# Last stage of a gated attention/SSM mix in 64 by 64 matmul tiles, and its tail ordered by a planner

## The chip, the cores and the metric

The kernel runs on one core of one Trainium2 chip. The metric is the device time of one execution in microseconds (us). Engines are called as in the profile: PE (TensorE matmuls; PEld are its weight loads), DVE (VectorE), ACT (ScalarE), POOL (GpSimd) and SP (SyncE); SP and POOL issue nearly all the transfers.

## The reference, cut to what matters

```python
g = sigmoid((x * gate_w).sum(-1, keepdims=True))    # one gate per token
a = local_dilated_attention(x, wqkv, wo)            # 32 heads, window 8, step 2
# b: per channel, a convolution over the 2048 tokens with a kernel K of that channel
K = einsum("dn,dnl,dn->dl", C, exp(dt*A*l), dt*B).real
y = irfft(rfft(pad(x)) * rfft(pad(K)))[:2048]
b = y + x * Dskip
out = g * a + (1 - g) * b                           # 2048 tokens x 640 channels, bf16
```

## The kernel before

The first part, to 299 us of the profiled span, computes the attention, stores `g*a` in device memory (`gaS`) and `1-g` (`omS`), makes K and the first half of the Fourier transforms of K and x. Its tasks are ordered by `Plan` (L69): each task has an engine, an estimated duration, inputs (`deps`), buffer slots that it takes and gives back (`acq`, `rel`) and a due time; `order()` plays them through and `emit()` records the instructions of each engine in that order.

The second part, `fft_conv` (L988), was written in program order. It multiplies the spectra and transforms back, all by matmuls with constant matrices:

- **Products** (L1013 to L1042), eight blocks of four frequencies. Per block four groups of eight matmuls give the real and imaginary part of both spectra into `fp` (L1023, two PSUM buffers of four banks); ACT evicts each into `sp_*` (L1026); DVE forms the complex product with six operations of 1280 elements per partition, four multiplications into `ta` and `tb_` and two additions into `Y` (L1036 to L1042). In the last block the imaginary part goes in three pieces of 16, 32 and 32 columns, so that the next stage can begin. SP loads the constants PSI and the input `gaF`; a two-element copy on POOL that reads a spectrum (L1004) holds each of the first loads back.
- **First inverse step** (`inv`, L1050): 20 results `cp` of 16 matmuls on 64-row tiles, alternately copied by ACT (L982) and DVE (L984) into `C`.
- **Last stage** (L1068 to L1090): 16 results `yp`. A partition is one of four channel groups (160 channels) times 32 tokens; a result holds four token steps. Per step two matmuls on the whole array, 128 x 160 (L1076). Then `(1-g)` scales: on DVE for six results (L1081), on ACT for ten, in four ACTIVATEs each (L1086). DVE adds `g*a` (L1087). Two results make an output tile `ot` (four buffers), stored by four transfers of 32 partitions in rows of 160 channels, 320 B (L1090).

DVE's order in the last stage, as recorded, is three scalings, eight adds, three scalings, eight adds. The results of both stages share four PSUM slots of two banks (tag `cy`). Two engines never read one result there.

Of the kernel before, what the change touches and what calls it, by code (L numbers as in the profile page):

```python
# [10 lines left out]
ACT = mybir.ActivationFunctionType  # L11
# [57 lines left out]
class Plan:  # L69
# [3 lines left out]
             "at": 2, "asb": 2, "pv": 2, "oT": 1, "ga": 1, "prj": 4, "prjw": 3, "pc": 4}  # L73
# [133 lines left out]
class Attn:  # L207
# [45 lines left out]
    def plan_gate(self, pl, cst, pa, g_sb, late):  # L253
# [25 lines left out]
        def twice(_):  # L279
            b["om2"] = cst.tile([16, 128, 2], BF16, name="om2")  # L280
            nc.scalar.activation(b["om2"][:], b["gz"][0:16, 1, 0:128].unsqueeze(2).to_broadcast([16, 128, 2]), ACT.Identity)

        def store(_):
            nc.gpsimd.dma_start(self.omS.rearrange("(i p) t -> i (p t)", p=128), b["om2"][:].rearrange("i p t -> i (p t)"))
# [5 lines left out]
        w = pl.add("gtwice", "A", 0.35, twice, deps=[u], rel=[("ar", m)], due=d)  # L290
# [621 lines left out]
def _fft_consts():  # L912
# [6 lines left out]
    for g in range(4):  # L919
        f1b[g, :, g, :] = f1c.reshape(32, 64)  # L920
# [14 lines left out]
    psis = np.zeros((32, 4, 64, 2, 4, 32), np.float32)  # L935
    for g in range(4):
        psis[:, g, :, 0, g, :] = Psi.real.transpose(1, 0, 2)
        psis[:, g, :, 1, g, :] = -Psi.imag.transpose(1, 0, 2)
    psis = psis.reshape(128, 64, 2, 128)
# [3 lines left out]
def fft_prefetch(ctx, tc, x, omS):  # L943
# [6 lines left out]
    P["omF"] = pre.tile([128, 64, 2], BF16, name="omF")  # L950
# [20 lines left out]
    def gates(g):  # L971
        nc.gpsimd.dma_start(P["omF"][32 * g:32 * g + 32], omS.rearrange("(a b) t -> a b t", b=64))
# [15 lines left out]
def fft_conv(ctx, tc, P, big, Bu, gaS, out2d):  # L988
# [4 lines left out]
    Bk = bufA[:].rearrange("p (c f q g) -> p c f q g", c=NCH, f=64, q=8)  # L993
    sb = ctx.enter_context(tc.tile_pool(name="ff_sb", bufs=1))
    Y = sb.tile([128, 2, 80, 128], BF16, name="Y")
    yv = Y[:].rearrange("p r x (f g) -> p r x f g", g=4)
    om32 = sb.tile([128, 64], F32, name="om32")
    psr = ctx.enter_context(tc.tile_pool(name="ff_psr", bufs=1))
    psis = []

    def load_psi(k, pool, after=None):
        t = pool.tile([128, 8, 2, 128], BF16, name=f"PSI{k}")
        if after is not None:
            nc.gpsimd.tensor_copy(t[:, 0, 0, 0:2], after)  # L1004
        nc.sync.dma_start(t[:], psi_d[:, 8 * k:8 * k + 8])
        psis.append(t)
    with big:
        nc.vector.tensor_copy(om32[:], omF[:, :, 0])
        gaF = P["pool"].tile([128, 64, 160], BF16, name="gaF", tag="uga")
        gr = gaS.rearrange("(a b) d -> a b d", b=64)  # L1010
        phis = P["phis"]
        with tc.tile_pool(name="ff_wk", bufs=2, side="right") as wk, tc.tile_pool(name="ff_ps2", bufs=2, space=PSUM) as ps2:
            for fb in range(8):  # L1013
                spec = {}
                PHI = phis[fb]
                for nm, B in (("k", Bk), ("u", Bu)):
                    for ro in range(2):
                        fp = ps2.tile([128, 4, 512], F32, name="fp")
                        for fl in range(4):
                            f1 = 4 * fb + fl  # L1020
                            for ri in range(2):
                                kind = (0 if ri == 0 else 2) if ro == 0 else (1 if ri == 0 else 0)
                                nc.tensor.matmul(fp[:, fl, 0:320].rearrange("p (c x) -> p c x", x=32), PHI[:, fl, kind, :],  # L1023
                                                 B[:, :, 2 * f1 + ri].rearrange("p c q g -> p c (q g)"), start=(ri == 0), stop=(ri == 1))
                        t = wk.tile([128, 80, 4, 4], BF16, name=f"sp_{nm}{ro}")
                        nc.scalar.activation(t[:], fp[:, :, 0:320].rearrange("p f (x g) -> p x f g", g=4), ACT.Identity)  # L1026
                        spec[(nm, ro)] = t
                if fb + 3 < 8:
                    phis.append(P["load_phi"](fb + 3))
                if fb < 4:  # L1030
                    load_psi(fb, psr, spec[("u", 1)][:, 0, 0, 0:2])
                    nc.sync.dma_start(gaF[32 * fb:32 * fb + 32], gr[:, :, 160 * fb:160 * fb + 160])
                ur, ui, kr, ki = spec[("u", 0)], spec[("u", 1)], spec[("k", 0)], spec[("k", 1)]
                ta = wk.tile([128, 80, 4, 4], BF16, name="ta")
                tb_ = wk.tile([128, 80, 4, 4], BF16, name="tb_")
                nc.vector.tensor_tensor(ta[:], ur[:], kr[:], ALU.mult)  # L1036
                nc.vector.tensor_tensor(tb_[:], ui[:], ki[:], ALU.mult)
                nc.vector.tensor_tensor(yv[:, 0, :, 4 * fb:4 * fb + 4, :], ta[:], tb_[:], ALU.subtract)
                for x0, x1 in (((0, 16), (16, 48), (48, 80)) if fb == 7 else ((0, 80),)):
                    nc.vector.tensor_tensor(ta[:, x0:x1], ur[:, x0:x1], ki[:, x0:x1], ALU.mult)  # L1040
                    nc.vector.tensor_tensor(tb_[:, x0:x1], ui[:, x0:x1], kr[:, x0:x1], ALU.mult)
                    nc.vector.tensor_tensor(yv[:, 1, x0:x1, 4 * fb:4 * fb + 4, :], ta[:, x0:x1], tb_[:, x0:x1], ALU.add)  # L1042
    C = bufA[:].rearrange("p (x d) -> p x d", d=160)
    with tc.tile_pool(name="ff_ps3", bufs=4, space=PSUM) as ps3, tc.tile_pool(name="ff_psr2", bufs=1, side="right") as psr2, \
            tc.tile_pool(name="ff_wk2", bufs=4, side="right") as wk2:
        for k in range(4, 8):
            load_psi(k, psr2)
        cps = {}

        def inv(cb, ro):  # L1050
            if ro == 0:
                cps[cb] = ps3.tile([128, 2, 4, 128], F32, name="cp", tag="cy")
            cp = cps[cb]
            for l in range(4):
                for c2 in range(2):
                    nc.tensor.matmul(cp[:, c2, l, :], Y[64 * c2:64 * c2 + 64, ro, 4 * cb + l, :],
                                     GAB[64 * c2:64 * c2 + 64, ro, :], start=(ro == 0 and l == 0), stop=(ro == 1), skip_group_check=True, tile_position=(64 * c2, 0))
            if ro == 1:
                dst = C.rearrange("p x (c q) -> p x c q", c=2)[:, :, :, 4 * cb:4 * cb + 4]
                copy_on(nc, 0 if cb == 9 else cb, dst, cp[:].rearrange("p c l x -> p x c l"))  # L1060
        for cb in range(4):
            inv(cb, 0)
        for cb in range(20):
            if cb >= 4:
                inv(cb, 0)
            inv(cb, 1)
        orr = out2d.rearrange("(a b) d -> a b d", b=64)
        for tb8 in range(8):  # L1068
            tt = wk2.tile([128, 8, 160], BF16, name="tt")
            ot = wk2.tile([128, 8, 160], BF16, name="ot")  # L1070
            for hh in range(2):
                yp = ps3.tile([128, 2, 512], F32, name="yp", tag="cy")
                for l in range(4):
                    t2 = 8 * tb8 + 4 * hh + l
                    for ro in range(2):
                        nc.tensor.matmul(yp[:, l // 2, 160 * (l % 2):160 * (l % 2) + 160], psis[tb8][:, 4 * hh + l, ro, :], C[:, 64 * ro + t2, :],  # L1076
                                         start=(ro == 0), stop=(ro == 1))
                t0 = 8 * tb8 + 4 * hh
                th = tt[:, 4 * hh:4 * hh + 4]
                if (2 * tb8 + hh) % 5 in (1, 3):  # L1080
                    nc.vector.tensor_tensor(th.rearrange("p (a b) (d t) -> p a b d t", b=2, t=2),  # L1081
                                            yp[:, :, 0:320].rearrange("p a (b d t) -> p a b d t", b=2, t=2),
                                            omF[:, t0:t0 + 4, :].rearrange("p (a b) t -> p a b t", b=2).unsqueeze(3).to_broadcast([128, 2, 2, 80, 2]), ALU.mult)
                else:
                    for l in range(4):
                        nc.scalar.activation(th[:, l], yp[:, l // 2, 160 * (l % 2):160 * (l % 2) + 160], ACT.Identity, scale=om32[:, t0 + l:t0 + l + 1])  # L1086
                nc.vector.tensor_tensor(ot[:, 4 * hh:4 * hh + 4], th, gaF[:, t0:t0 + 4, :], ALU.add)  # L1087
            for g in range(4):
                eng = (nc.sync, nc.gpsimd, nc.sync, nc.scalar if tb8 == 7 else nc.gpsimd)[g]
                eng.dma_start(orr[:, 8 * tb8:8 * tb8 + 8, 160 * g:160 * g + 160], ot[32 * g:32 * g + 32])  # L1090
# [182 lines left out]
```

## Time and profile before

| | us |
|---|---|
| time of 3 runs | 378.54, 380.16, 382.12 (median 380.16) |
| profiled execution, its own time | 382.15 |
| its span | 380.4 |
| busy: PE, DVE, ACT, POOL | 319.4, 323.0, 307.8, 92.6 |
| blocks of products begin | 299.1 |
| last input spectrum evicted | 342.1 |
| copies of the first inverse step | 345.5 to 357.7 |
| first matmul of the last stage | 357.8 |
| first store issued, last store issued | 363.6, 374.7 |

The span counts from the first to the last instruction; the time of the execution is 1.75 us longer. "Busy" of PE is of pipelined matmuls, whose durations overlap: the pitch of a matmul (the length of a row of n matmuls by n) is its cost, not its duration.

### The profile page before, as it was taken

To read this page: it belongs to the slowest core of one execution; us is meant where nothing else is said; L and a number is where in the kernel's file an instruction comes from. 1 tells how busy PE (TensorE), PEld (TensorE's weight loads), DVE (VectorE), ACT (ScalarE), POOL (GpSimd) and SP (SyncE) were. 2 spreads that over 40 slices of the span, in tenths; PEclk is the share of its full clock that TensorE was granted. 3 is DMA by queue.
4 is the path that set the end of the run, shared out by engine and by line. 5 is a ranking of instruction groups with operands and counts; after the bars stand their busy time and mean duration, and the time that the engine had idled before them with its cause. 6 is when DMAs were issued, how large, how long until landed. Compare 5 with 4: busy or idle time off the path is not lost.

```text
span 380.4 us, 11537 instructions
## 1 busy us (share of the span) xinstructions
PE 319.4 (84%) x4938; PEld 190.8 (50%) x4966; DVE 323.0 (85%) x435; ACT 307.8 (81%) x433; POOL 92.6 (24%) x122
## 2 busy tenths in 40 slices
PE   0259999998999999979898989999999899978760
PEld 0135663533454455444444535566777665547750
DVE  4788999768999788998999998999896299999772
ACT  1598884489998889898989879987986799995890
POOL 8930341130103031573520201000010022000053
PEclk9998999999999999986969989999999999998995
DMA  8991898671426359426647733222461299915056
GB/s 264 371 254 36 254 277 243 167 242 57 149 68 194 125 138 244 107 56 152 153 103 211 252 96 113 73 73 58 161 209 36 67 202 234 234 15 214 2 138 142
DMA packets 51528, 58.83 MB, mean 155 GB/s; under 512 B 36244, under 2 KB 43284, under 8 KB 51220
## 3 DMA queue, kind: packets, MB, share of 16 engines
q1 hardware_dynamic: 41492, 28.78, 28.6%
q0 software_dynamic: 8256, 28.69, 25.7%
q8 instruction: 39, 0.64, 0.7%
q10 hardware_dynamic: 1728, 0.61, 0.7%
q14 instruction: 13, 0.11, 0.1%
HBM read 38.29 MB, written 19.77 MB: 153 GB/s over the span
## 4 chain that ended last, share of the span: by engine, by line
PE 29%; ACT 16%; DVE 7%; issue 3%; POOL 1%; DMA 1%; POOLq 0%; ACTq 0%; DVEq 0%
PE tb L449 6%; PE fp L1023 5%; PE bp L1194 5%; ACT big L784 5%; PE tb L466 4%; PE ar L772 3%; ACT sp_u L1026 3%; DVE bufA L984 3%; ACT sp_k L1026 3%; PE kps L825 2%; PE yp L1076 2%; ACT big L786 1%; ACT bufA L784 1%; POOL out_dram L1090 1%; DVE prod L379 1%
## 5 line engine op out<-in xcount | busy, mean ns | idle before, releaser
L330 PE MATMUL tb<-bufA 128*128 128x512 bf16 x283 | 71.6, 389 | 4.5 <-DVE bufA L494 2.0
L772 PE MATMUL ar<-Rarg,L 64*128 64x304 bf16 (+1 forms) x480 | 56.0, 289 | 10.5 <-ACT big L784 4.2
L784 ACT ACTIVATE big<-ar 128x608 bf16<-128x608 int16 x96 | 58.3, 682 | 3.2 <-PE ar L772 2.6
L786 ACT ACTIVATE big<-ar 128x864 bf16<-128x864 f32 x60 | 49.4, 895 | 1.2 <-PE ar L772 1.0
L444 DVE TENSOR_TENSOR pv<-vc,asb 128x2048 bf16<-128x2048 bf16 x40 | 47.4, 1220 | 3.3 <-PE tb L449 3.3
L379 DVE TENSOR_TENSOR prod<-qc,kc 128x2048 bf16<-128x2048 bf16 x40 | 47.5, 1220 | 3.1 <-PE lg L385 3.1
L330 PEld LDWEIGHTS <-bufA 128*128 128x128 bf16 x300 | 33.2, 120 | 31.9 <-issue 7.4
L772 PEld LDWEIGHTS <-L 64*128 64x128 bf16 x480 | 22.0, 95 | 41.7 <-issue 37.2
L449 PE MATMUL tb<-pv,ident 128*128 128x512 bf16 (+1 forms) x181 | 39.7, 357 | 1.0 <-issue 0.5
L825 PE MATMUL kps<-qq,pt 128*32 128x22 bf16 (+1 forms) x2560 | 37.0, 174 | 1.7 <-issue 1.5
L825 PEld LDWEIGHTS <-pt 128*32 128x32 bf16 (+1 forms) x2560 | 25.1, 93 | 25.5 <-issue 17.1
L1023 PEld LDWEIGHTS <-PHI 128*128 128x128 bf16 x256 | 24.8, 97 | 17.6 <-issue 7.4
L466 PE MATMUL tb<-wo_sb,oT 128*128 128x320 bf16 x160 | 28.0, 307 | 0.0
L492 ACT ACTIVATE prj<-tb 128x512 bf16<-128x512 f32 x27 | 16.0, 598 | 13.4 <-PE tb L330 13.0
L449 PEld LDWEIGHTS <-ident 128*128 128x128 bf16 x192 | 18.1, 101 | 14.4 <-issue 2.2
L1026 ACT ACTIVATE sp_k<-fp 128x1280 bf16<-128x1280 f32 x16 | 19.1, 1236 | 3.3 <-PE fp L1023 3.3
L809 DVE TENSOR_TENSOR qq<-big 128x1408 bf16<-128x1408 bf16 x24 | 21.2, 885 | 0.0
L245 PE MATMUL ar<-ident,xn 128*128 128x128 bf16 x80 | 7.9, 263 | 15.9 <-DMA xn<-in_A_x_dram 14.2
L1023 PE MATMUL fp<-bufA,PHI 128*128 128x320 bf16 x128 | 19.1, 298 | 2.2 <-ACT sp_u L1026 1.5
L1023 PE MATMUL fp<-big,PHI 128*128 128x320 bf16 x128 | 19.2, 298 | 1.8 <-ACT sp_k L1026 1.8
L1026 ACT ACTIVATE sp_u<-fp 128x1280 bf16<-128x1280 f32 x16 | 19.1, 1237 | 1.8 <-PE fp L1023 1.8
L370 POOL DMA_DIRECT2D vc<-vS x8 | 7.0, 880 | 48.2 <-DVE pv L444 39.5
(198 smaller groups left out, 610.0 us busy)
## 6 DMA issues: line engine op xcount, KB each, us to landing
asb<-aS SPq DMA_DIRECT2D x8, 512.0 KB, 4.0
PSI<-c_psi SPq DMA_DIRECT2D x8, 512.0 KB, 6.0
PHI<-c_phi POOLq DMA_DIRECT2D x8, 384.0 KB, 5.7
Sprm<-pc SPq DMA_DIRECT2D x12, 240.0 KB, 7.8
L<-Sprm SPq DMA_DIRECT2D x80, 36.0 KB, 2.6
kc<-kS POOLq DMA_DIRECT2D x8, 337.5 KB, 6.2
vc<-vS POOLq DMA_DIRECT2D x8, 337.5 KB, 5.6
xn<-in_A_x_dram SPq DMA_DIRECT2D x4, 640.0 KB, 11.7
```

What stands on the lines that cost most here:

```text
L330: nc.tensor.matmul(ppf, self.wq[:, kt, which * D + e:(which + 1) * D:5], self.xT[:, c0 // 1024, kt, c0 % 1024:c0 % 1024 + SC], start=(kt = ...
L379: nc.vector.tensor_tensor(b[e][:], b["qc"][:, e, :].unsqueeze(1).to_broadcast([128, W, C]), win(b["kc"][:, e, :], 0, W, DIL, C), ALU.mult)
L444: nc.vector.tensor_tensor(b["pv", e][:, :, k, :].rearrange("p w (b t) -> p w b t", t=64), for_e, aw, ALU.mult)
L449: nc.tensor.matmul(b["op", e][:, 0:n, :], ident[:], b["pv", e][:, w, 0:n, :], start=(w == 0), stop=(w == W - 1))
L466: nc.tensor.matmul(apf[:, :320], b["oT"][:, e, i * 128:(i + 1) * 128], wo_sb[:, e, hf * 320:(hf + 1) * 320], start=(e == 0), stop=(e == 4))
L772: nc.tensor.matmul(ar[:, g2, a0:a0 + ncol], L[rows, sb, gp, l0:l0 + 128], R[rows, c0:c0 + ncol], start=True, stop=True, tile_position=(64 ...
L784: nc.scalar.activation(dst[:, 2 * gp:2 * gp + 2, sub, :], ar[:].bitcast(I16)[:, :, 0:2 * SW:2], ACT.Sin, scale=SCL)
L786: nc.scalar.activation(dst[:, 2 * gp:2 * gp + 2].rearrange("p g s n -> p g (s n)"), ar[:, :, 0:2 * EW], ACT.Exp)
L809: nc.vector.tensor_tensor(qq[:], trg[:, :, KI:].rearrange("p a (v m) -> p a v m", v=2), exq[:, :, KI:].unsqueeze(2).to_broadcast([128, 32, ...
L825: nc.tensor.matmul(kps[32 * g:32 * g + 32, h, NM * ql:NM * ql + NM], pt[rows, k, v, :], qq[rows, k, v, :], start=(g not in started), stop= ...
L1023: nc.tensor.matmul(fp[:, fl, 0:320].rearrange("p (c x) -> p c x", x=32), PHI[:, fl, kind, :], B[:, :, 2 * f1 + ri].rearrange("p c q g -> p ...
L1026: nc.scalar.activation(t[:], fp[:, :, 0:320].rearrange("p f (x g) -> p x f g", g=4), ACT.Identity)
```

## The change

The last stage works on 64 by 64 tiles. A partition is now one of two token halves (of 32 steps each) times two channel halves times 32 tokens, and the two groups of 160 channels of a half lie in the two banks of a result: 32 token steps with 320 channels per partition instead of 64 steps with 160. A step takes eight matmuls of 64 rows, 64 columns and 160 moving elements, on the four 64 by 64 tiles of the array. The constants are half as large (one tile `psi`), and the rows of `omS`, `gaF` and of the output change with it: an output row is now 320 channels, 640 B. For this the order of the four channel groups in the constant F1c is permuted, `Y` is laid out with the group ahead of the frequency, and the eviction of `fp` reads the four frequencies of a column, which lie in four banks, one after another.

A result has three steps (the last has two; there are 11), with four slots. For its first step DVE scales and adds in one operation, out of PSUM; for the other steps ACT scales, one ACTIVATE of 320 elements per step, and DVE adds both in one operation. An output tile holds two results, but results 0, 9 and 10 have one each; it is stored by two transfers of SP and two of POOL.

In the products, both multiplications with the real part of the input come first, then the two with the imaginary part, each followed by its addition; in the last block these go in the three pieces. All of `fft_conv` is made of tasks of the planner, which chooses the engine of the 20 copies (ACT or DVE) too. The gate `1-g` is no longer stored twice per token. The recorded order of the first part stays as it was.

```diff
-            nc.scalar.activation(b["om2"][:], b["gz"][0:16, 1, 0:128].unsqueeze(2).to_broadcast([16, 128, 2]), ACT.Identity)
+            nc.scalar.activation(b["om2"][:], b["gz"][0:16, 1, 0:128], ACT.Identity)
...
-        f1b[g, :, g, :] = f1c.reshape(32, 64)
+        f1b[g, :, (0, 2, 1, 3)[g], :] = f1c.reshape(32, 64)
...
-    yv = Y[:].rearrange("p r x (f g) -> p r x f g", g=4)
+    yv = Y[:].rearrange("p r x (g f) -> p r (x g) f", g=4)
...
+    pl = Plan(free=dict(P=0.0, A=0.0, D=0.0, S=0.0, G=0.0), phase=0.0, look=0.0, ba=0.0, bd=0.0, grace=0.0, warm=1)
...
-                        t = wk.tile([128, 80, 4, 4], BF16, name=f"sp_{nm}{ro}")
-                        nc.scalar.activation(t[:], fp[:, :, 0:320].rearrange("p f (x g) -> p x f g", g=4), ACT.Identity)
+                t = wk.tile([128, 320, 4], BF16, name=f"sp_{nm}{ro}")
+                evict(nc, en, t[:], spec[nm, ro][:, :, 0:320].rearrange("p f x -> p x f"))
...
+        for ro in range(2):
+            last = pl.add(f"ta{fb}{ro}", "D", 0.81, lambda _, f=mul, ro=ro: f(_, 0, 80, f"ta{ro}", ("u", 0), ("k", ro)), deps=[sp["u", 0], sp["k", ro]], after=[last], due=d - 1)
+            heads.append(last)
+        for k, (x0, x1) in enumerate(((0, 16), (16, 48), (48, 80)) if fb == 7 else ((0, 80),)):
+            w = 0.04 + 0.0096 * (x1 - x0)
+            for ro in range(2):
+                p1 = pl.add(f"tc{fb}{k}{ro}", "D", w, lambda _, f=mul, x=(x0, x1), ro=ro: f(_, x[0], x[1], "tc", ("u", 1), ("k", 1 - ro)), deps=[sp["u", 1], sp["k", 1 - ro]], after=[last], due=d + k)
+                last = pl.add(f"Y{fb}{k}{ro}", "D", w, lambda _, f=add, x=(x0, x1), ro=ro: f(_, x[0], x[1], ro), deps=[heads[ro], p1], due=d + k)
...
+        cps.append(pl.add(f"cp{cb}", "AD", {"A": 1.0, "D": 1.18}, ev, deps=ms, rel=[("cy", ms[0])], due=60 + cb))
+    for n, w in enumerate((3,) * 10 + (2,)):
...
-                        nc.tensor.matmul(yp[:, l // 2, 160 * (l % 2):160 * (l % 2) + 160], psis[tb8][:, 4 * hh + l, ro, :], C[:, 64 * ro + t2, :],
-                                         start=(ro == 0), stop=(ro == 1))
+            for k, v in enumerate(vs):
+                for ro in range(2):
+                    for j in range(2):
+                        for h in range(2):
+                            nc.tensor.matmul(yp[64 * j:64 * j + 64, h, 160 * k:160 * k + 160], psi[64 * h:64 * h + 64, 32 * j + v, ro, :], C[64 * h:64 * h + 64, 64 * ro + 32 * j + v, :],
+                                             start=(ro == 0), stop=(ro == 1), skip_group_check=True, tile_position=(64 * h, 64 * j))
...
-                        nc.scalar.activation(th[:, l], yp[:, l // 2, 160 * (l % 2):160 * (l % 2) + 160], ACT.Identity, scale=om32[:, t0 + l:t0 + l + 1])
-                nc.vector.tensor_tensor(ot[:, 4 * hh:4 * hh + 4], th, gaF[:, t0:t0 + 4, :], ALU.add)
+        def scale(_, v, k, n=n, part=part):
+            nc.scalar.activation(q["tt", n][:, k - 1, :].rearrange("p (h d) -> p h d", h=2), part(k), ACT.Identity, scale=om32[:, v:v + 1])
+        def mix(_, n=n, vs=vs, o=o, k0=k0):
+            nc.vector.tensor_tensor(o["t"][:, k0 + 1:k0 + w, :], q["tt", n][:, 0:w - 1, :], gaF[:, vs[1]:vs[0] + w, :], ALU.add)
+        def both(_, v=vs[0], o=o, k0=k0, part=part):
+            nc.vector.scalar_tensor_tensor(o["t"][:, k0, :].rearrange("p (h d) -> p h d", h=2), part(0), om32[:, v:v + 1], gaF[:, v, :].rearrange("p (h d) -> p h d", h=2), ALU.mult, ALU.add)
...
-                eng.dma_start(orr[:, 8 * tb8:8 * tb8 + 8, 160 * g:160 * g + 160], ot[32 * g:32 * g + 32])
+                for h in range(2):
+                    j = (0, 2)[e == "G"] + h
+                    (nc.sync if e == "S" else nc.gpsimd).dma_start(orr[j // 2, j % 2][:, o["v"]:o["v"] + o["n"], :], o["t"][32 * j:32 * j + 32, 0:o["n"]])
```

The lines of the changed kernel that the prediction names: L1021 (matmuls of `fp`), L492 and L494 (evictions and copies by the common helper `evict`, L490), L1048 and L1051 (multiplications, additions into `Y`), L1075 (`cp`), L1105 (`yp`), L1114 (ACT's scaling), L1118 and L1121 (DVE's add and its combined operation), L1132 (stores).

More of the change, by code (lines that the diff above doesn't have):

```diff
@@ L289, in plan_gate @@
         u = pl.add("gturn", "P", 0.1, turn, deps=[v], due=d, eq=20)
-        w = pl.add("gtwice", "A", 0.35, twice, deps=[u], rel=[("ar", m)], due=d)
+        w = pl.add("gtwice", "A", 0.25, row, deps=[u], rel=[("ar", m)], due=d)
         pl.add("gst", "G", 0.55, store, deps=[w], due=d, dma=0.4)
@@ L949, in fft_prefetch @@
     P["GAB"] = pre.tile([128, 2, 128], BF16, name="GAB")
-    P["omF"] = pre.tile([128, 64, 2], BF16, name="omF")
+    P["omF"] = pre.tile([128, 32], BF16, name="omF")
     P["pace"] = pre.tile([128, 2], BF16, name="pace")
@@ L993, in fft_conv @@
     Bk = bufA[:].rearrange("p (c f q g) -> p c f q g", c=NCH, f=64, q=8)
+    C = bufA[:].rearrange("p (x d) -> p x d", d=160)
     sb = ctx.enter_context(tc.tile_pool(name="ff_sb", bufs=1))
     Y = sb.tile([128, 2, 80, 128], BF16, name="Y")
-    yv = Y[:].rearrange("p r x (f g) -> p r x f g", g=4)
[L997 to L1024, printed above, removed]
-                        t = wk.tile([128, 80, 4, 4], BF16, name=f"sp_{nm}{ro}")
-                        nc.scalar.activation(t[:], fp[:, :, 0:320].rearrange("p f (x g) -> p x f g", g=4), ACT.Identity)
-                        spec[(nm, ro)] = t
-                if fb + 3 < 8:
-                    phis.append(P["load_phi"](fb + 3))
[L1030 to L1042, printed above, removed]
@@ new lines, in fft_conv @@
+    yv = Y[:].rearrange("p r x (g f) -> p r (x g) f", g=4)
+    om32 = sb.tile([128, 32], F32, name="om32")
+    psi = sb.tile([128, 64, 2, 64], BF16, name="psi")
+    nc.vector.tensor_copy(om32[:], omF[:])
+    gaF = P["pool"].tile([128, 32, 320], BF16, name="gaF", tag="uga")
+    gr = gaS.rearrange("(a j v) (e c) -> j e a v c", j=2, v=32, e=2)
+    orr = out2d.rearrange("(a j v) (e c) -> j e a v c", j=2, v=32, e=2)
+    phis, q = P["phis"], {}
+    a, b, c = ExitStack(), ExitStack(), ExitStack()
@@ new lines, in fft_conv, with inv, ev @@
+    cps, prev = [], None
+    for cb in range(20):
+        ms = []
+        for ro in range(2):
+            def inv(_, cb=cb, ro=ro):
+                if cb == 0 and ro == 0:
+                    b.close()
+                    q["ps"] = c.enter_context(tc.tile_pool(name="ff_ps3", bufs=4, space=PSUM))
+                if ro == 0:
+                    q["cp", cb] = q["ps"].tile([128, 2, 4, 128], F32, name="cp")
+                for l in range(4):
+                    for c2 in range(2):
+                        nc.tensor.matmul(q["cp", cb][:, c2, l, :], Y[64 * c2:64 * c2 + 64, ro, 4 * cb + l, :],
+                                         GAB[64 * c2:64 * c2 + 64, ro, :], start=(ro == 0 and l == 0), stop=(ro == 1), skip_group_check=True, tile_position=(64 * c2, 0))
+            prev = pl.add(f"inv{cb}{ro}", "P", 0.27, inv, deps=[muls[cb, ro]], after=ends + [prev], acq=["cy"] if ro == 0 else [], due=60 + cb + 0.1 * ro)
+            ms.append(prev)
+        def ev(en, cb=cb):
+            evict(nc, en, C.rearrange("p x (c q) -> p x c q", c=2)[:, :, :, 4 * cb:4 * cb + 4], q["cp", cb][:].rearrange("p c l x -> p x c l"))
+        cps.append(pl.add(f"cp{cb}", "AD", {"A": 1.0, "D": 1.18}, ev, deps=ms, rel=[("cy", ms[0])], due=60 + cb))
```

136 lines of the change are left out of this document (84 added, 52 removed).

## Prediction

> **What bounds the kernel now.** The page's chain of waits comes first. TensorE (PE) leads with 29% of the span and no line has more than 6%, so only the stage that is edited can be costed. The table by stage comes next. It splits the tail into products, copies, first half of the results, second half, and drain:
>
> ```profile
> core 0: us, PE busy (x) PEld busy (x) DVE busy (x) ACT busy (x) POOL busy (x), PEclk, DMA share, GB/s
> 299.00:342.10 43.10, 38.35 (x256) 24.78 (x256) 34.72 (x44) 38.30 (x32) 6.05 (x9) 1.00 0.80 165
> ...
> 345.50:357.80 12.30, 9.97 (x278) 9.06 (x274) 11.44 (x13) 10.37 (x11) 0.00 (x0) 0.88 0.18 69
> 357.80:364.20 6.40, 6.25 (x88) 6.14 (x89) 3.95 (x7) 5.62 (x21) 0.01 (x1) 1.00 0.00 0
> 364.20:374.10 9.90, 3.09 (x40) 2.75 (x39) 7.42 (x16) 5.97 (x21) 7.50 (x13) 0.92 0.82 193
> ```
>
> To 342.1 PE and ACT alternate and DVE is slack. Then the copies fill DVE and ACT. In the results stage no engine is full (DVE 11.4 of 16.3 us), and nothing is stored in its first 6.4 us. The groups of that stage give the prices (count | busy, mean ns):
>
> ```profile
> L1086 ACT ACTIVATE tt<-yp,om 128x160 bf16<-128x160 f32 x40 | 11.6, 469 | 2.7 <-PE yp L1076 2.7
> ...
> L982 ACT ACTIVATE bufA<-cp 128x1024 bf16<-128x1024 f32 x11 | 10.4, 1045 | 4.2 <-PE cp L1056 4.2
> L984 DVE CAST bufA<-cp 128x1024 bf16<-128x1024 f32 x9 | 10.4, 1217 | 0.7 <-PE cp L1056 0.7
> ...
> L1087 DVE TENSOR_TENSOR ot<-tt,gaF 128x640 bf16<-128x640 bf16 x16 | 6.8, 486 | 1.8 <-ACT tt L1086 1.4 <-issue 0.4
> L1081 DVE TENSOR_TENSOR tt<-yp,omF 128x640 bf16<-128x640 f32 x6 | 4.9, 823 | 3.2 <-PE yp L1076 3.2
> ```
>
> The chain in order of time shows what ended last:
>
> ```profile
> 351.90 5.79 DVE bufA L984 x5
> ...
> 357.83 6.26 PE yp L1076 x88
> ...
> 367.59 4.34 DMA out_dram<-ot
> ...
> 374.12 0.58 POOL out_dram L1090
> ```
>
> The 4.34 us is DVE waiting to refill an output tile whose old content is still being stored. The rest comes from the timeline (start, length, instruction, idle before and its releaser), at the end of the products and, in a second piece, in the middle of the kernel:
>
> ```profile
> 340.92 0.83 DVE L1036 TENSOR_TENSOR ta<-sp_u,sp_k 128x1280 bf16<-128x1280 bf16 x1
> ...
> 342.11 0.83 DVE L1037 TENSOR_TENSOR tb__6373<-sp_u,sp_k 128x1280 bf16<-128x1280 bf16 x1 [0.36 <-ACT sp_u L1026]
> ...
> 345.46 1.94 ACT L982 ACTIVATE bufA<-cp 128x1024 bf16<-128x1024 f32 x2 [3.39 <-PE cp L1056]
> ```
>
> ```profile
> 225.69 0.39 PE L385 MATMUL lg<-prod,ind 128*32 128x512 bf16 x4
> ...
> 227.01 0.37 PE L825 MATMUL kps<-qq,pt 64*32 64x22 bf16 x32
> ```
>
> After the last input spectrum (342.1) five full-size products pass before DVE is free, and ACT idles 3.39 us. The last two rows, matmuls on tiles of 32 columns, are used below. Landmarks of this execution: DVE's last copy ends 357.7, its last add 374.06, the last store is issued at 374.70, the queue's own wait for it ends near 378.1, span 380.4.
>
> **The change part by part.** Up to 299 the order of every engine is unchanged; the gate's ACTIVATE is half as wide and its transfers a half and a quarter of the size, with no one waiting: nothing.
>
> *Blocks 0 to 6 (299 to 341).* The same 32 groups of matmuls and 32 evictions, one of each every 1.31 us, set the pace. The eviction now hops PSUM bank at every element instead of every fourth. No row does that. The nearest are L982 and L984, which hop 512 B at every element and a bank at every fourth: eight ACT ones in 7.44 us, 0.93 each, where 1024 elements at 0.83 ns (rows L492: 512 in 0.598, 1024 in 1.023) are 0.85. I take nothing; the other end is a doubled element, over 30 us. DVE's two adds per block now write runs of 4 elements, formerly 16. L984 writes such runs from PSUM at 1.217, and the same copy with runs of 16 (L494) takes 1.22, so at one element a cycle they cost nothing. At two a cycle no row shows them: bounds 0 and 0.67 (1280 elements at L984's pace, 1024 in a pitch of 1.153, would be 1.42, less today's pitch of 0.745). I take 0, by that row. A block then costs DVE 2 x 0.745 + 4 x 0.86 = 4.9 us (a product that waits for the one before takes 0.86), inside its 5.25. Cover: 0.33 us. Beside this, four of SP's eight constant loads go, its input loads become eight of half the size, and POOL gets eight more two-element copies in front of them (0.83 each, row L1004) after each block's constant load (0.55); POOL has 5.25 us per block, and the last load is issued near 343, 20 us before its use: nothing.
>
> [...]
>
> *Last block and copies.* The second product no longer waits for 342.1: it ends at 342.4, and after it come four quarter-size steps chained by one buffer (0.31 each), so both halves of piece one are out at 343.6, formerly 344.85. PE's 16 matmuls and the eviction follow, and ACT starts at 344.2 instead of 345.46. But the built order puts two of DVE's eight copies between the later pieces, which end at 346.4 and 349.1 instead of 345.9 and 346.7. DVE: 344.8 + 8 x 1.153 + 1.6 for the interposed products + about 0.6 of waits = 356.2. ACT: 344.2 + 12 x 0.93 + 0.9 of waits for slots and pieces = 356.2. Formerly 357.7: **1.6 us saved** (bounds 0.9 to 2.2).
>
> *Matmuls of the results.* 256 on 64x64 tiles replace 128 of 71 ns (88 in 6.26). No row has 64 columns. Nearest: four 128x32 tiles of 512 columns within 0.39 us (L385; one after another they would need 0.85), and L1056's two row tiles, 144 in 4.95, 34 ns at a duration above 200. So tiles run side by side; side by side four share today's 71, 18 ns each, L1056's pitch scaled by 160/128 is 43. I take 25, 0.6 us per result. PE is then no bound; the ends move the end by -0.2 and +0.6.
>
> *Reading the results.* ACT: 40 x 0.288 becomes 21 x 0.421 (0.288 plus 160 elements at 0.83 ns; isolated 0.54, row L475). DVE: 6 x 0.775 + 16 x 0.411 = 11.2 becomes 11 of a new combined scale-and-add, plus 10 adds at 0.411 and a short one. The combined one is priced by L477 (320 from PSUM, 0.547): pitch 0.44, ends 0.44 and 0.55; 9.3 in all. By sums alone the stage would take 10.5 us. It won't: every result tile is now read by both engines, and the built program lets them read in turn only. For results 1 to 6 DVE reads first, then ACT twice, then the add behind the next combined one: ACT cannot start before DVE ends, which gives 2.03 us for two. For results 0 and 7 to 10 the order is ACT, DVE, ACT: 0.55 + 0.56 + 0.42 + two semaphores of 0.04 = 1.61 each, and the add of the result before waits behind the combined one on DVE. So from the first matmul at 356.2: ACT at 357.0, DVE at 357.6; result 1 at 358.1; five of about 1.03 to 363.3; 2.04 until result 7 (365.3), for which ACT first finishes result 6; two of 1.61 (368.5); 1.61 to result 10 (370.1); last add ends 370.9. That is 14.7 us, formerly 16.2: **1.5 us saved** (semaphores of 0.02 or 0.08 move it by -0.4 and +0.7, the combined one's upper end by +0.5).
>
> *Stores.* 4096 pieces of 640 B instead of 8192 of 320 B, first store at 359.5 instead of 363.6, four output tiles refilled seldom enough that the 4.34 us wait is gone. Even at today's 193 GB/s they would all be through by 374.6. The end: after the last add the two small stores of result 9 still stand ahead on SP and POOL (0.58 each on POOL), so the last issue is 372.5, 1.65 after the add, formerly 0.65: **1.0 lost**. The landing took 3.4 us behind a full queue; 41 KB behind a queue under half full should take 2.6 (row: minimum 2.2): **0.8 saved** (bounds 0 and 1.2).
>
> Sum: 1.6 + 1.5 - 1.0 + 0.8 = 2.9 us saved. The span of 380.4 becomes 377.5 and this execution's own 382.15 becomes 379.25. It stands 2.0 above the median of the runs, 380.16, which becomes **377.3**.
>
> **The rivals.**
> 1. *Tiles do not run side by side.* Loading weights of 64 columns is about half of 98 ns (row L1076, 128 columns); if loads go one at a time, 49 ns a matmul; if nothing overlaps, 71. PE then paces the results: 1.4 or 5.4 us more, 378.7 to 382.7. Against it: L385, L1056. [...]
> 2. *Slower: the short runs halve the adds to Y.* 0.67 x 2 per block against 0.33 of cover: 1.0 us by eight blocks = 8, less 2.9: 385.3. It decides from an add of about 1.17 us on (2 x 0.35 less the cover, eight times, is 2.9). For it: no row of two a cycle with such runs. Against: L984.
> 3. *Slower: the four-bank eviction.* ACT is without slack, so each 0.1 us costs 3.2; past 1.33 us instead of 1.24 the gain is gone; at 1.5 it is 385.7. Against: L982.
> 4. *The transfers set the end* and the gain is swallowed: 379.5 to 380. For it: DMA share 0.8 to 1.0 today. Against: half the pieces, and four us earlier.
>
> **How the numbers follow.** Forecast 0.64 (own range 375.9 to 379.0), rival 1 0.14, rival 2 0.08, rival 3 0.08, rival 4 0.06. One per cent is 3.8 us, about what a measurement of this kernel can tell from no change: faster than 376.4 needs the good ends together (semaphores, matmuls, landing: -1.0), a quarter of the forecast's share, 0.16. Slower than 384.0 is rival 2 and most of rival 3, 0.14. Within 1%: 0.70. The range 375.3 to 383.0 takes in rivals 1 and 4 and leaves out 2, most of 3 and the luckiest runs.
>
> **What would show it.** Eviction L492 of fp at 1.24 us and adds to Y (L1051) at 0.83: if not, rivals 3 or 2. First ACT copy near 1.3 us earlier against the last eviction. Matmuls to yp (L1105) at 17 to 35 ns of pitch. In the results stage DVE and ACT idle on each other, worst in results 7 to 10 at 1.6 us each; if these come at 0.9 the turn-taking is not what I think, and the gain is nearer 5. I am wrong also if the stores' landing stays at 3.4 us.

## The result, and the profile after

| | before | changed |
|---|---|---|
| time, median of 20 runs each | 382.28 us (378.54 to 386.28) | 379.68 us (376.68 to 382.87) |
| ratio | | 0.9938 (95% interval 0.9914 to 0.9962) |
| ratio, second job | | 0.9882 (0.9828 to 0.9936) |
| profiled executions: span | 380.4, 380.4 | 375.1, 374.3 |

The change is a gain of 0.6%, in a second job (run after_again) 1.2%. Ratios, here and below, are of the runs within 1.5% of their kernel's fastest, which leaves 18 of the changed kernel's 20 and, below, four of own_7's six. The three runs of before that the prediction had were low ones: their median was 380.16, the medians of four jobs were 381.2 to 383.2.

To compare traces, times are counted from E, the end of the last eviction of an input spectrum (342.07 before, 340.42 in the changed kernel). What lies ahead of E scatters: in the twelve profiled executions of kernels that all share the changed kernel's first part or nearly so, the first eviction started anywhere from 298.0 to 303.4 us. What lies behind E repeats to 0.2 us in the changed kernel and 0.4 in before. So the spans' difference of 5.3 us is not the change; the difference behind E is. (From the first eviction's start to E it is 41.65 and 41.68 us before, 41.75 and 41.76 in the changed kernel: nothing is won there.) Rows that end at the end of the span are good to 0.05 us, since spans are given to 0.1.

| from two profiled executions each, us | before | changed | saved | forecast |
|---|---|---|---|---|
| E to first matmul of yp | 15.76, 15.71 | 14.40, 14.38 | 1.35 | 1.6 |
| first matmul of yp to last add | 16.23, 15.96 | 14.52, 14.50 | 1.6 | 1.5 |
| last add to end of the last issue | 1.21, 1.37 | 2.36, 2.34 | -1.05 | -1.0 |
| that to the end of the span | 5.13, 4.86 | 3.40, 3.30 | 1.65 | 0.8 |
| E to the end of the span | 38.33, 37.90 | 34.68, 34.52 | 3.5 | 2.9 |

The groups of the changed kernel (count | busy, mean ns of one | idle before, releaser) answer the prices that the prediction had to guess:

```profile
L492 ACT ACTIVATE sp_u<-fp 128x1280 bf16<-128x1280 f32 x16 | 19.4, 1236 | 1.6 <-PE fp L1021 1.2
...
L1051 DVE TENSOR_TENSOR Y<-ta,tc 128x1280 bf16<-128x1280 bf16 x14 | 11.6, 826 | 0.5
...
L1114 ACT ACTIVATE tt<-yp,om 128x320 bf16<-128x320 f32 x21 | 9.8, 524 | 4.1 <-DVE ot L1121 3.0 <-PE yp L1105 1.0
...
L1105 PE MATMUL yp<-bufA,psi 64*64 64x160 bf16 x256 | 6.1, 231 | 4.3 <-ACT tt L1114 3.0 <-DVE bufA L494 1.3
L1121 DVE SCALAR_TENSOR_TENSOR ot<-yp,om,gaF 128x320 bf16<-128x320 f32 x11 | 5.9, 547 | 3.8 <-ACT tt L1114 2.2 <-issue 1.6
```

The eviction that hops a bank at each element takes 1.236 us, the same as before (L1026: 1.236 and 1.237), and the adds to Y in 8-byte runs 0.826 (before 0.824 to 0.827). The last three rows carry the reading of the stage: PE idles on ACT, ACT on DVE (3.0 us) and DVE on ACT (2.2 us). The chain, in order of time, shows how, from result 7 on:

```profile
363.86 0.56 DVE ot L1121
...
364.46 0.40 issue
364.87 0.53 ACT tt L1114
...
365.42 0.56 DVE ot L1121
...
366.43 0.53 ACT tt L1114
...
366.99 0.56 DVE ot L1121
```

The piece called issue is ACT's second scaling of result 7, and the ACT piece is its first of result 8: the timeline has the two from 364.44 on, 0.95 us together. So one result takes ACT, DVE and ACT again one behind the other, 1.56 us each.

### The profile page after: what moved, and what is told of

It is laid out like the page before. It is cut to its first block, busy times and chain, and to the rows that moved or that the text cites. A ratio compares the mean times of both kernels' runs of the same rounds, so it can differ in the third digit from the quotient of the medians.

```text
span 375.1 us, 11789 instructions
## 1 busy us (share of the span) xinstructions
PE 315.3 (84%) x5066; PEld 186.9 (50%) x5094; DVE 320.1 (85%) x436; ACT 307.3 (82%) x415; POOL 95.7 (26%) x129
## 5 line engine op out<-in xcount | busy, mean ns | idle before, releaser
L330 PE MATMUL tb<-bufA 128*128 128x512 bf16 x283 | 71.2, 388 | 4.5 <-DVE bufA L494 2.3
L330 PEld LDWEIGHTS <-bufA 128*128 128x128 bf16 x300 | 33.2, 120 | 31.6 <-issue 6.8
L825 PE MATMUL kps<-qq,pt 128*32 128x22 bf16 (+1 forms) x2560 | 36.8, 174 | 0.7 <-issue 0.6
L825 PEld LDWEIGHTS <-pt 128*32 128x32 bf16 (+1 forms) x2560 | 25.0, 93 | 23.9 <-issue 15.3
L1021 PEld LDWEIGHTS <-PHI 128*128 128x128 bf16 x256 | 24.8, 97 | 17.7 <-issue 8.3
L492 ACT ACTIVATE prj<-tb 128x512 bf16<-128x512 f32 x27 | 16.0, 598 | 13.8 <-PE tb L330 13.4
L466 PE MATMUL tb<-wo_sb,oT 128*128 128x320 bf16 x160 | 27.2, 300 | 0.0
L492 ACT ACTIVATE sp_k<-fp 128x1280 bf16<-128x1280 f32 x16 | 19.4, 1236 | 3.0 <-PE fp L1021 2.5
L1021 PE MATMUL fp<-bufA,PHI 128*128 128x320 bf16 x128 | 19.4, 298 | 2.1 <-ACT sp_u L492 1.2
L1021 PE MATMUL fp<-big,PHI 128*128 128x320 bf16 x128 | 19.5, 298 | 1.6 <-ACT sp_k L492 1.3
L492 ACT ACTIVATE sp_u<-fp 128x1280 bf16<-128x1280 f32 x16 | 19.4, 1236 | 1.6 <-PE fp L1021 1.2
L968 POOL COPY pace<-Usb 32x2 bf16<-32x2 bf16 x7 | 13.2, 1883 | 23.9 <-DMA Usb<-in_A_x_dram 23.9
```

Source lines behind the costliest of these rows:

```text
L330: nc.tensor.matmul(ppf, self.wq[:, kt, which * D + e:(which + 1) * D:5], self.xT[:, c0 // 1024, kt, c0 % 1024:c0 % 1024 + SC], start=(kt = ...
L466: nc.tensor.matmul(apf[:, :320], b["oT"][:, e, i * 128:(i + 1) * 128], wo_sb[:, e, hf * 320:(hf + 1) * 320], start=(e == 0), stop=(e == 4))
L492: nc.scalar.activation(o, i, ACT.Identity)
L825: nc.tensor.matmul(kps[32 * g:32 * g + 32, h, NM * ql:NM * ql + NM], pt[rows, k, v, :], qq[rows, k, v, :], start=(g not in started), stop= ...
```

## The experiments

Theory: the last stage is paced by the two readers' turns at a shared result tile (as built, ACT and DVE read one tile in turn only; in the changed kernel's first trace each turn at a result begins 0.03 to 0.10 us after the end of the turn before it). Rivals: TensorE's small tiles, the reuse of output buffers, or the transfers pace it. A second question is whether the order of the products made the earlier start. All kernels but before_again were made from the changed one. The last four columns (us) are from one profiled execution each; E to yp is 0.4 shorter where PE kept its full clock (last section), so ends are compared from the first matmul of yp where this differs. The ratios of the variants differ by less than their intervals, mostly; it is the traces that tell the variants apart.

| kernel | ratio to before (95%) | E to yp | yp to last add | issues end after add | E to span's end |
|---|---|---|---|---|---|
| dve_first | 0.9883 (0.9851 to 0.9915) | 14.00 | 14.08 | 1.35 | 32.94 |
| dve_first_7 | 0.9879 (0.9835 to 0.9922) | 13.99 | 13.41 | 1.57 | 32.62 |
| own_tiles | 0.9891 (0.9841 to 0.9940) | 14.41 | 11.62 | 2.54 | 32.25 |
| own_7 | 0.9813 (0.9758 to 0.9869) | 14.00 | 10.21 | 3.76 | 31.78 |
| own_7_stores | 0.9841 (0.9783 to 0.9899) | 14.38 | 10.20 | 3.36 | 31.63 |
| own_7_early | 0.9823 (0.9795 to 0.9851) | 14.00 | 10.09 | 3.71 | 30.88 |
| own_7_half | one run | 14.40 | 10.22 | 2.52 | 29.56 |
| after_half | one run | 13.99 | 14.50 | 1.35 | 32.27 |
| old_products | 0.9964 (0.9924 to 1.0004) | 15.76 | 14.52 | 2.36 | 36.00 |
| tile_by_tile | 0.9943 (0.9906 to 0.9980) | 14.40 | 14.87 | 2.35 | 35.03 |
| before_again | 0.9997 (0.9970 to 1.0024) | 15.71 | 15.96 | 1.37 | 37.90 |

**The turns: DVE first.** `dve_first` makes each of ACT's scalings wait, in the plan, for DVE's combined operation of the same result:

```diff
-            tts.append(pl.add(f"tt{n}{k}", "A", 0.44, ..., deps=[m], acq=...
+            tts.append(pl.add(f"tt{n}{k}", "A", 0.44, ..., deps=[m], after=[os[-1]], acq=...
```

> Only the order in which ACT and DVE may read one result tile is changed: DVE is always first, also for results 0 and 7 to 10; no engine's own order of instructions changes. If turn-taking on a shared result tile paces the last stage, results 7 to 10 come every 1.0 us as results 1 to 6 do, instead of every 1.57: the stretch from the first matmul of yp to the last add falls from 14.5 to about 12.2 us (11.8 to 12.7), and the time by about 2 us against the changed kernel. If TensorE, the reuse of output tiles or the stores pace these four results, the stretch stays within 0.3 us of 14.5. The part before the last stage is the same program as in the changed kernel, so where the first input spectrum's eviction starts (298.7 in the changed kernel's trace, 300.4 in the trace before) shows only the scatter of the first part.

The stage took 14.08, not 12.2. Yet results 2 to 9 came 0.99 us apart, as expected, where 7 to 9 had been 1.56 apart. DVE's timeline shows what was late next (start, length, idle before and its releaser):

```profile
365.22 0.55 DVE L1121 SCALAR_TENSOR_TENSOR ot<-yp,om,gaF 128x320 bf16<-128x320 f32 x1
...
366.84 0.49 DVE L1118 TENSOR_TENSOR ot<-tt,gaF 128x640 bf16<-128x640 bf16 x1 [0.44 <-ACT tt L1114]
367.90 0.55 DVE L1121 SCALAR_TENSOR_TENSOR ot<-yp,om,gaF 128x320 bf16<-128x320 f32 x1 [0.57 <-DMA out_dram<-ot]
369.11 0.33 DVE L1118 TENSOR_TENSOR ot<-tt,gaF 128x320 bf16<-128x320 bf16 x1 [0.65 <-ACT tt L1114]
```

Result 10 waits for an output tile that is still being stored, and stands behind the add of result 9, which waits for ACT. The next kernel takes the first away.

**Output buffers.** `dve_first_7` gives the seven output tiles a buffer each:

```diff
+                q["ot"] = ctx.enter_context(tc.tile_pool(name="ff_ot", bufs=7, side="right"))
-                o["t"] = q["wk"].tile([128, 6, 320], BF16, name="ot")
+                o["t"] = q["ot"].tile([128, 6, 320], BF16, name="ot")
```

> DVE always reads a result first, and the seven output tiles have a buffer each instead of four shared ones. With four buffers DVE waited 0.57 us (1.6 us behind its work) at result 10 for the transfer of an old output tile, and the stretch from the first matmul of yp to the last add was 14.08 us instead of the 12.2 that turn-taking gave. If that wait alone hid the gain, the stretch is 12.2 to 12.6 us now, with results every 1.0 us to the end. If the gain was hidden by something else, it stays at 13.8 to 14.2.

13.41: the DMA's wait is gone, and the expectation missed by 0.8 us and more. The combined operation of result 9 began at 367.33 and that of result 10 at 369.36, 2.03 later instead of 1.0, because DVE's own order puts the add of result 9 (which waits for ACT) ahead of it and ACT may no longer begin result 10 by itself. In the changed kernel it could. The fixed turn helps results 7 to 9 and costs the last.

**No turns.** `own_tiles` gives DVE's step and ACT's steps of a result a PSUM tile each, two slots of each:

```diff
-            yp = q["yp", n] = q["yps"].tile([128, 2, 512], F32, name="yp")
+            fill("yp", vs[:1], n)
...
+        m = prev = pl.add(f"ya{n}", "P", 0.20 * (w - 1), lambda _, f=fill, vs=vs: f("ya", vs[1:]), after=[prev], acq=["ya"], due=100 + n)
```

> Each result is split in two PSUM tiles, one read by DVE only and one by ACT only, two slots each, so that no tile is read by both engines. If turn-taking is the cause, both engines run at the sum of their own work, 0.95 us per result: first matmul of yp to last add 11.3 us (10.8 to 12.0) instead of 14.5, and the time 2.5 to 3.3 us under the changed kernel's. If only the wrong order in results 7 to 10 costs, and the turn-taking as such nothing, it is as with DVE always first, about 12.2. If stores or TensorE pace the stage, 14.2 to 14.8; if two slots instead of four starve the engines, 13 or more with waits of both on yp's matmuls.

11.62, as the theory said, and 2.9 us less than the changed kernel with the engines' operations all kept. One wait of 1.19 us is left, again for an output tile:

```profile
366.59 0.55 DVE L1125 SCALAR_TENSOR_TENSOR ot<-yp,om,gaF 128x320 bf16<-128x320 f32 x1 [1.19 <-DMA out_dram<-ot]
```

`own_7` adds the seven buffers (the edit above):

> Own result tiles for DVE and ACT, and seven output buffers. The wait of 1.19 us for an output tile at result 7 should be gone: first matmul of yp to last add 10.4 to 10.8 us instead of 11.62, about the 10.5 that the engines' own sums give. If the wait only hides another one behind it (two slots of each result tile, TensorE), 11.2 or more. The end of the span moves less than the last add, since the last issues on POOL already ended 2.5 us after it and one of these takes 0.56 us: last add to the end of the issues 2.5 to 3.5 us.

10.21, slightly under the 10.5 of the engines' sums: turns and buffers together cost the changed kernel 4.3 us of its 14.5. Its groups show that both engines now hardly wait:

```profile
L1119 ACT ACTIVATE tt<-ya,om 128x320 bf16<-128x320 f32 x21 | 8.9, 591 | 1.0 <-PE ya L1109 1.0
...
L1126 DVE SCALAR_TENSOR_TENSOR ot<-yp,om,gaF 128x320 bf16<-128x320 f32 x11 | 5.9, 544 | 0.8 <-PE yp L1109 0.8
```

Counted from the first matmul of yp, the end of the span gained only 2.4 to 2.5 us (17.78 instead of 20.28 and 20.14). The rest went into the issues, which now end 3.76 us after the last add.

**Issues or transfers?** `own_7_stores` hands result 9's four stores to ACT:

```diff
-            for e, t_ in (("S", 1.3), ("G", 1.1)):
+            for e, t_ in (("A", 1.0), ("A", 1.0)) if n == 9 else (("S", 1.3), ("G", 1.1)):
```

> As with own tiles and seven buffers, but the four stores of result 9 are issued by ACT, which has then nothing left to do, and SP and POOL keep those of result 10. If the end is set by the queue of issues behind the last add, the issues end 1.2 to 1.6 us after the last add instead of 2.4 or more, and the span from the last input spectrum's eviction is about 1 us shorter than with own tiles and seven buffers. If the transfers themselves set it, the time between the last issue and the span's end grows by as much and the span stays within 0.3 us.

3.36 instead of 3.76. Counted from E the end is within 0.2, but this execution had the half clock and own_7 the full one; from the first matmul of yp it comes at 17.24 instead of 17.77, 0.5 us earlier, between both expectations. So issuing is a part of it, and not the whole. `own_7_early` puts the short result first, and DVE's add of result 0 ahead of result 2, so that storing begins earlier:

```diff
-    for n, w in enumerate((3,) * 10 + (2,)):
+    for n, w in enumerate((2,) + (3,) * 10):
...
+        os.append(pl.add(f"st{n}", "D", 0.47, both, deps=[m], after=[mix0] if n == 2 else [], ...
```

> Own result tiles and seven output buffers, with the short result (two steps) first instead of last, and DVE's add of result 0 ahead of its work on result 2, so that the first store is issued about 0.9 us earlier against the first matmul of yp (2.65 us before). If the transfers set the end, the span from the last input spectrum's eviction is 0.3 to 0.9 us shorter than the 31.8 with own tiles and seven buffers. If the engines set it, it is 0 to 0.5 us longer, since the last result has a step more.

0.9 us shorter behind E, though the last add moved by 0.12 only and both had the full clock: the transfers set most of the end. Three lines on `own_7` go with it: its DMA engines' busy tenths and rate, from 358 to 371 in 40 slices, and SP's issues (minimum/median/maximum ns):

```profile
DMA  0004469288469869989697999798999989797971
GB/s 0 0 0 110 99 168 230 75 158 225 172 211 242 173 156 173 294 276 298 197 223 254 256 238 336 203 335 246 250 227 270 275 260 278 209 290 227 286 219 45
```

```profile
L1138 SPq DMA_DIRECT2D out_dram<-ot x14: 316/482/2159, 358.3 to 369.1; - x14
```

In the changed kernel's first trace no issue of SP took over 0.47 us:

```profile
L1132 SPq DMA_DIRECT2D out_dram<-ot x14: 315/414/467, 358.0 to 370.3; - x14
```

The medians, 482 and 414 ns, and own_7's last five issues, of 0.50 to 1.19 us, bear on the load, though a 16 KB packet of the DMA's instruction queue was in flight beside two of these. The longest one, 2.16, need not: such a packet was in flight beside it too (last section), and the changed kernel's second trace has an issue like it, of 1.47 us.

`own_7_half` and `after_half` leave POOL's stores out:

```diff
-            for e, t_ in (("S", 1.3), ("G", 1.1)):
+            for e, t_ in (("S", 1.3),):
```

> Own result tiles and seven output buffers, without POOL's stores: the second token half of the output is not written. If the transfers have become the bound there, SP's issues no longer wait for room in the queue (14 of them end within 1.5 us of the last add instead of 3.76), and the span from the last input spectrum's eviction is 28.3 to 29.5 us instead of 31.8. If issuing itself is slow, SP's 14 issues still end 3 us or more after the last add and the span is over 30.5.

Against the first matmul of yp, which takes the clock out, the end came at 15.16 instead of 17.78 us. SP's issues still end 2.52 after the last add, not 1.5, so that part of the expectation missed (that issues wait for room in a queue was the author's guess, and no trace shows it); one of the last six took 1.31 us instead of about 0.41, with an instruction packet in flight, and that is 0.9 of the 1.0. Of the 2.6 us, 1.2 lie in SP's issues and 1.4 behind the last of them. The last packet lands 13.57 us after the first matmul of yp instead of 15.67, so with half the output to store, the same adds and the same 14 issues on SP, it is there 2.1 us earlier.

> The changed kernel without POOL's stores: the second token half of the output is not written. It shows what the transfers cost there. If they are hidden and only the issues behind the last add count, the end follows SP's last issue, which came 0.9 us ahead of POOL's: the span from the last input spectrum's eviction is 33.4 to 34.0 us instead of 34.5 to 34.7. If the transfers set the end, half of them are gone and it is 32.5 or less.

Against the first matmul of yp the end came at 18.28 instead of 20.14 to 20.28. SP's last issue ends 1.0 earlier than POOL's did, and 0.9 us more are gone behind it: between both expectations. In the changed kernel the transfers don't set the pace; the end waits for POOL's last ones. The packets in the traces split the 0.9: the last one lands 0.83 us after the last issue instead of 1.21, which is 0.4, and the span ends 1.57 after it instead of 2.1 to 2.2, where POOL now has nothing to wait for.

**The products.** `old_products` puts the old order of the six operations back:

```diff
-        for ro in range(2):
-            last = pl.add(f"ta{fb}{ro}", ...)
+        for ro, k, x0, x1 in [(0, 0, 0, 80)] + [(1, k, x0, x1) for k, (x0, x1) in enumerate(...)]:
+            last = pl.add(f"ta{fb}{k}{ro}", ...)
```

> The order of the six product operations of a block is put back to that of the kernel before (real part complete, then imaginary part), all else as in the changed kernel. If the new order is what lets the first inverse step begin early, ACT's first copy starts 3.4 us after the last input spectrum's eviction instead of 2.27, the first matmul of yp comes 1.0 to 1.5 us later against that eviction (15.4 to 15.9 us instead of 14.4), and the time is 1.0 to 1.5 us above the changed kernel's. If the pairing of copies by the planner made the gain, the first matmul of yp stays within 0.4 us of 14.4.

The first matmul of yp is back at E + 15.76, where the kernel before has it (15.76, 15.71), and the rest is as in the changed kernel. ACT's idle time ahead of its first copy, of the changed kernel and of this one:

```profile
342.69 1.02 ACT L492 ACTIVATE bufA<-cp 128x1024 bf16<-128x1024 f32 x1 [2.27 <-PE cp L1075]
```

```profile
344.70 1.94 ACT L492 ACTIVATE bufA<-cp 128x1024 bf16<-128x1024 f32 x2 [3.00 <-PE cp L1074]
```

The order makes the 1.35 us; nothing is seen that the planner's choice of engines for the copies would add. (The first copy came at E + 3.00 and not at the expected 3.4, but the first matmul of yp did not come earlier for it.)

**The small tiles.** `tile_by_tile` changes only the order of the matmuls:

```diff
-            for k, v in enumerate(vs):
-                for ro in range(2):
-                    for j in range(2):
-                        for h in range(2):
+            for j in range(2):
+                for h in range(2):
+                    for k, v in enumerate(vs):
+                        for ro in range(2):
```

> Only the order of the eight matmuls per step is changed: all matmuls of one 64 by 64 tile of a result (six) come one after another, instead of a change of tile at every matmul. If neighbours on different tiles run side by side and neighbours on one tile do not, the pitch of the yp matmuls rises from 20 to 25 ns (24 in 0.61 us, 96 in 1.97) to 50 to 71 ns, 24 take 1.2 to 1.7 us, TensorE paces the last stage and first matmul to last add is 15 to 18 us instead of 14.5. If the pitch of 25 ns has nothing to do with tiles running side by side, it stays at 20 to 30 ns and the time is the changed kernel's.

The first two rows are of the changed kernel (PEld are the weight loads), the third is of this one:

```profile
354.79 1.82 PEld L1105 LDWEIGHTS <-psi 64*64 64x64 bf16 x97 [1.43 <-issue]
354.82 1.97 PE L1105 MATMUL yp<-bufA,psi 64*64 64x160 bf16 x96 [1.29 <-DVE bufA L494]
```

```profile
359.57 9.48 PE L1105 MATMUL yp<-bufA,psi 64*64 64x160 bf16 x256 [1.28 <-DVE bufA L494]
```

1.97 by 96 is 20.5 ns, where one matmul's own duration is 231 ns (row L1105 of the groups above), so they overlap. The third row can't be divided so: it runs through all eleven results and holds the pauses between them. By the starts in the trace, its first 96 matmuls begin within 2.87 us, 30 ns apart (1.74 and 18 in the changed kernel), and the 24 of a later result within 0.85 us, 37 ns apart (0.38 to 0.39 and 17). So side by side counts, but six in a row on one tile cost less than the 50 to 71 expected, and TensorE is nearly hidden either way (stage 14.87 instead of 14.52, not the 15 to 18 expected).

**Before, once more.**

> The kernel before once more, with a trace. If its last part is rigid too, the span from the last input spectrum's eviction is 38.3 us again (38.1 to 38.5), and the end of the last issue to the end of the span 5.1 us, against 3.4 in the changed kernel; the start of the first input spectrum's eviction scatters. If those 5.1 us were an accident of one trace, they come as 3.4 to 4.5 now, and the changed kernel's gain in the last part is nearer 2.5 us than 3.7.

4.86 and 37.90: the long end is no accident.

## Why the prediction was right or wrong

Three of the four terms came within 0.25 us, by the mechanisms that were forecast; the fourth, the landing, followed another queue than the one it was read from. The number failed at one step: "It stands 2.0 above the median of the runs, 380.16, which becomes 377.3". The sum against the execution's own time was 379.25, and the median of the changed kernel is 379.68. The 2.0 us were taken as this execution's excess; they were the scatter of three runs. With 20 runs the median of before is 382.28, which is where the profiled execution stood (382.15). Counted as a difference, 2.9 us were forecast, and 382.28 less 379.68 is 2.6. That these lie so close is partly luck: the terms measured below sum to 3.5, and the second job's 1.2% is some 4.5 us. Where between 2.6 and 4.5 the medians settle stays open, since the part ahead of E scatters by 5 us.

- *Last block and copies*, 1.6: 1.35. The copy began at E + 2.27 instead of 2.1, since PE ran its first matmuls at half clock (last section); where it kept the full clock the copy began at E + 2.05 and the term was 1.7 (15.71, also at full clock, less 14.00). The two interposed copies and the overall course were as read from the built order.
- *Matmuls*, 25 ns: 20.5 in a long row, 25 in rows of 24 (0.61 us). Rival 1 is out. Its loads one at a time, 49 ns each (an estimate, half of the 98 of row L1076), do not agree with a pitch of 20.5. The trace gives a load 106 ns on average and has 97 of them in 1.82 us, 19 ns apart, so they overlap. So they did on 32 columns in before: the matmuls of the prediction's row L825 have their 32 loads, about 93 ns each, within 0.27 us. And in a row matmuls of 512 columns on the whole array start 0.215 us apart in before's trace (L330), 0.86 for the four that L385 has within 0.39.
- *Reading the results*, 14.7 us: 14.5. Results 7 to 10 took 1.56 each for 1.61. That it was the turns is shown by dve_first, where they came 0.99 apart, and by own_tiles.
- *Stores*, -1.0 for the issues behind the last add: -1.05.
- *Landing*, 0.8: 1.65, the one term that was mis-sized. The prediction read SP's wait (to about 378.1), but POOL's queue drained last. POOL's own rows at the end, of before and of the changed kernel (minimum/median/maximum ns, first and last start):

```profile
L1268 POOLq DRAIN  x3: 46/171/4672, 374.5 to 380.1; - x3
```

```profile
L1313 POOLq DRAIN  x3: 46/103/3334, 371.0 to 374.9; - x3
```

  The longest is the first of the three: it ends at 379.2 and 374.3, 3.9 and 2.6 us after POOL's last issue, 1.3 saved. The last packet of POOL's queue had landed at 377.8 and 372.9, so the 1.3 lies in the landing itself (2.5 us after the last issue, then 1.2); the end of that drain follows the landing by 1.4 in both, and by 1.3 to 1.5 in all twelve traces in which POOL stores. The other 0.4 lies in the closing steps behind it (1.2 and 0.8 us), and its cause stays open.
- *Adds to Y and the eviction*, costed at nothing: 826 and 1236 ns, so rivals 2 and 3 are out. One and two elements a cycle are the prediction's names for two rates of the rows, 1.19 ns an element (L984, 1024 in 1.217 us) and 0.65 (the adds, 1280 in 0.826); at the second, too, runs of 4 elements cost nothing.
- *Transfers set the end* (rival 4): not in the changed kernel, but in the main once the turns are gone.

## What to carry to other kernels

Splitting one result between two engines pays more if each reads its own PSUM tile: here two tiles in place of one, the same banks in all, took 2.9 us off a stage of 14.5. When a wait is removed, ask what it had covered: here it was first the reuse of output buffers, then the transfers, and of 4.3 us won in the stage 2.4 reached the end. The best kernels of the study, own_7 and own_7_early, stand 1.8 to 1.9% under the kernel before, with intervals that reach into those of own_tiles and dve_first_7. And compare stages from a common event inside the trace, not the spans, when what lies ahead of it scatters by more than the change is worth; a median of three such runs is no level.

## What the hardware showed unexpectedly

**The clock right after E.** PE idles 2.24 us around E in the changed kernel (from E - 1.33 to E + 0.90), and in some executions its granted clock then falls to half (0.50). The two rows are the same stretch, E + 2 to E + 4, in the changed kernel and in own_7 (columns: busy time and count of PE, PEld, DVE, ACT, POOL, then clock, DMA share, GB/s):

```profile
342.42:344.42 2.00, 2.00 (x44) 2.00 (x42) 1.66 (x3) 1.11 (x2) 0.00 (x0) 0.50 0.52 138
```

```profile
343.62:345.62 2.00, 1.53 (x56) 1.36 (x50) 1.97 (x4) 1.94 (x3) 0.00 (x0) 1.00 0.50 137
```

The five executions with the new product order that kept the full clock reach the first matmul of yp at E + 13.99 or 14.00, the six others at 14.38 to 14.41: 0.4 us by chance. In each of the traces the granted clock changes only on a grid of 3.41 us, and near E no stretch of that grid was idle throughout. Laid on the grid, all 14 executions sort by how much of one stretch PE idled near E: 1.85 to 2.74 us in the eight that fell to half (2.24 in the changed kernel's first trace, 2.13 in before's), at most 1.82 in the six that kept the full clock. So here the clock goes with where the idle time lies in the grid; no run moved that alone. (That is a figure for this stretch: in the changed kernel's first trace PE idled 1.11 us from 187.73 to 191.14, a stretch of 76 matmuls, 64 of them of 22 columns, and the clock was 0.50 from there on.)

**Long issues and the instruction queue.** Nine of SP's issues of stores took over 1.2 us (1.24 to 2.16), in eight of the traces, and beside each of them a 16 KB packet of the DMA's instruction queue was in flight. Seven of them end 0.36 to 0.41 us after that packet landed, the length of an ordinary issue, as if the issue had waited for its instructions; the other two, in own_7_stores and own_7_early, 0.56 and 1.04 after it. That they wait for it is not shown by an experiment, but three of the nine are in the kernels that store half the output, so a crowded queue is not what they have in common.

**Two readers of one PSUM tile.** The waits between ACT and DVE are in the program as built. With them, none of the 21 readings by ACT overlaps DVE's reading of the same result in the changed kernel's first trace; what would happen without them, no run shows.
